# Eight instead of seven head pairs of a linear-attention and mixer kernel in plain float32

## The chip, the cores and the metric

The kernel runs on one core of one Trainium2 chip. The metric is the device time of one execution in microseconds (us). TensorE (PE, with its weight loads as PEld) multiplies matrices, VectorE (DVE), ScalarE (ACT) and GpSimd (POOL) work on elements, and SyncE (SP) issues most of the DMA transfers. Each engine goes through its own instructions in a fixed order; an instruction whose input is not there holds up everything behind it on that engine.

## The reference, cut to what matters

Eight batch entries of 576 tokens, eight heads of 64 channels each. First a linear attention:

```python
def phi(x):                                   # x: q or k, 64 channels per head
    proj = x @ w_phi                          # 64 -> 128 features
    proj = proj - max(abs(proj), axis=-1)     # per token
    return concat([exp(proj), exp(-proj)])    # 256 features
q_p, k_p = phi(q), phi(k)
kv, z = k_p.T @ v, sum(k_p, axis=tokens)
x = (q_p @ kv) / (q_p @ z + 1e-6)             # per head; heads side by side: 512 channels
```

Then a mixer over the result, one batch entry at a time: `u = x + (relu(x.T @ w_tok1) @ w_tok2).T` over the tokens (576 to 256 and back), and `u + relu(u @ w_ch1) @ w_ch2` over the channels (512 to 1536 and back).

## The kernel before

Heads are treated in pairs, two on the 128 partitions, so each batch entry has four pairs and there are 32 in all (0 to 31). Pairs 0 to 3 make up the first batch entry, pairs 4 to 7 the second one.

**Two precisions.** A pair with a number under `PLAIN` (L26) is made in plain float32, where each matmul of the program stands as two MATMUL instructions in the trace. The others are made from float32r parts: a value is written as a rounded high part and a low part (what is left), and a product is the sum of three float32r matmuls (`mm3`, L619 ff.). For such a pair the raw keys and queries are loaded as `raw` and stacked, high part on one half of the partitions, low part on the other (`stack`: ACT copies, POOL subtracts; tiles stk and stq). A projection of 128 tokens is then one matmul of 256 columns, whose halves ACT and DVE add up (tile part). A plain pair is loaded by two transfers of 256 and 320 KB into `pair` tiles (`load_plain`, L665), and a projection is one float32 matmul of 128 columns straight from them. Even pairs use the buffers k0 and k1, odd ones q0 and q1; there is one buffer of each, and stk and stq use the same four. So a plain pair's transfer waits until the pair two before it has been projected.

**Tiles of the attention.** ppk, ppq and ppt are the projections of keys, queries and the last 64 query tokens; mx their largest size, pm the difference, kp and qf the exponentials (qh, ql the parts of the latter). pkv is keys times values. The plain way (`add_kv`, L764) is eighteen matmuls of 104 or 130 columns that leave features on the partitions; the split way (`turn_kv`, L731) is twelve matmuls of 256 columns, a copy kf and four transposes pkt. pt are the transposed query features and pn the numerators and denominators: two matmuls per piece where plain, six where split. A piece is 320 or 256 tokens of one head; the name pn_01 says tokens of the first segment (0), second head (1). Then u is copied out; the denominators go through four small DMAs (few, inv, and u twice) with a reciprocal between them, and POOL multiplies u by u into xt, the input of the mixer.

**The mixer.** `token_mix` (L893) transposes xt (px), splits it (xh, xl), multiplies by w_tok1 (pa, then ah, al) and w_tok2 (ph), and adds to xt, in two halves h of 256 channels, two pairs each; pa_1 and ph_1 are those of the second half. `channel_stream` (L1009) works on blocks of 256 tokens: six rounds of 24 matmuls into h (L961) and 24 into acc (L976) each, 288 matmuls per block and 18 blocks. Blocks 0 and 1 lie inside the first batch entry; block 2 crosses into the second one and starts when that one's token mix is done.

**What sets the order.** Every operation is recorded first, then `arrange` (L275) places them on the engines with a table of costs: keys, queries and token mixing have urgency on TensorE, the channel stream is taken where nothing else is ready. So h and acc matmuls fill whatever the rest leaves.

**PSUM banks of the projections** (`less_max`, L631 ff.): from pair 4 on, keys of either kind use the bank keys. Queries that are split use three buffers with the tag rest; plain ones from the 19th tile on (`BORROWED = 18`) use the one bank h, which the channel stream's h uses too:

```python
elif base == 0 and (nplain["q"] % 2 == 0 or nplain["q"] >= BORROWED):
    ps = ps_h.tile([P, 2, 2, F], F32, tag="h", name=f"pp{name}")
elif kind == "k" or base == 0:
    ps = ps_w.tile([P, 2, 2, F], F32, tag="keys", name=f"pp{name}", bufs=1)
else:
    ps = ps_w.tile([P, 2, 2, F], F32, name=f"pp{name}", **REST)
```

All operations are recorded by one helper, so the profile gives nearly every instruction the line L174; tiles tell them apart.

Of the kernel before, what the change touches and what calls it, by code (L numbers as in the profile page):

```python
# [22 lines left out]
T = 256  # L23
E = 1536
NC_, NE, NT = C // P, E // P, T // P
PLAIN = 7  # L26
OPEN = 4
WIDE = 104
BORROWED = 18
# [449 lines left out]
def mixer_kernel(ctx, tc, qk, qkp, vals, w_phi, w1, w1t, w2, wc1, wc2d, out):  # L479
# [125 lines left out]
    def stack(raw, base, name):  # L605

        out = []
        lo = D - base
        for k, (c, n) in enumerate(((0, 512), (512, 640))):
            t = wk.tile([P, n], F32R, tag=f"{name[0]}{k}", name=f"st{name}{k}", bufs=1)  # L610
            src = raw[base:base + D, c:c + n]
            nc.scalar.copy(t[base:base + D], src)
            nc.gpsimd.tensor_tensor(t[lo:lo + D], src, t[base:base + D].bitcast(F32), op=ALU.subtract)
            out.append(t)
        return out
# [42 lines left out]
    def load(i):  # L658

        raw = wk.tile([P, 2 * S], F32, tag="raw", name=f"raw{i}", bufs=1)  # L660
        lo, hi = (D if i <= PLAIN else 0), (D if i == B * NP else P)
        nc.sync.dma_start(raw[lo:hi], qk[i, lo:hi])
        raws[i] = raw

    def load_plain(i):  # L665

        out = []
        for k, (c, n) in enumerate(((0, 512), (512, 640))):
            t = wk.tile([P, n], F32, tag=f"{'kq'[i % 2]}{k}", name=f"pair{i}{k}", bufs=1)
            nc.sync.dma_start(t, qkp[i, :, c:c + n])  # L670
            out.append(t)
        pairs[i] = out

    def keys():
# [3 lines left out]
        for i in range(B * NP):  # L678
            yield from until(lambda: i < 2 or i - 2 in asked)
            if i < PLAIN:  # L680
                load_plain(i)
# [3 lines left out]
            (nc.sync if i else nc.scalar).dma_start(v_sb.rearrange("p u j d -> p (u j d)"), vals[i])  # L685
            plain = D if i < PLAIN else None
            ts = pairs[i] if i < PLAIN else stack(raws[i], D, f"k{i}")
            for g, us in enumerate(groups if i < PLAIN else blocks):
                pm = less_max(ts, us, f"k{i}_{g}", plain)
# [98 lines left out]
    def sides(i):  # L788
        return (0, 1) if i < 2 * NP else (1, 0)

    def queries():
# [3 lines left out]
        for piece in pieces:  # L795
# [9 lines left out]
            if piece:  # L805
                i, k, j = piece
                if (k, j) == (sides(i)[0], 0):
                    plain = 0 if i < PLAIN else None
                    if i < PLAIN:
# [73 lines left out]
    def until(cond):  # L883
        while not cond():
            yield None
# [236 lines left out]
```

## Time and profile before

| what | value |
|---|---|
| median of three runs | 1110.08 us (1109.37 to 1110.85) |
| the profiled execution's own time | 1109.82 us |
| its span, first to last instruction | 1107.9 us |
| mean granted TensorE clock, share of full speed | 0.998 |
| busy share of the span: PE, PEld | 97%, 92% |
| busy share: DVE, ACT, POOL | 61%, 54%, 49% |
| MATMUL instructions | 8862 |
| last 150 us, from about 950 us on | h and acc alone, PE busy without a break |

A busy TensorE in the profile is not one at its peak: the end of a matmul is modelled and reaches into the next, so that a short break does not show as idle time. How many matmuls start in a stretch, and how far apart, tells more. In the trace float32 matmuls count twice.

### The profile page before, as it was taken

To read this page: it belongs to the slowest core of one execution; us is meant where nothing else is said; L and a number is where in the kernel's file an instruction comes from. 1 tells how busy PE (TensorE), PEld (TensorE's weight loads), DVE (VectorE), ACT (ScalarE), POOL (GpSimd) and SP (SyncE) were. 2 spreads that over 40 slices of the span, in tenths; PEclk is the share of its full clock that TensorE was granted. 3 is DMA by queue.
4 is the path that set the end of the run, shared out by engine and by line. 5 is a ranking of instruction groups with operands and counts; after the bars stand their busy time and mean duration, and the time that the engine had idled before them with its cause. 6 is when DMAs were issued, how large, how long until landed. Compare 5 with 4: busy or idle time off the path is not lost.

```text
span 1107.9 us, 23729 instructions
## 1 busy us (share of the span) xinstructions
PE 1078.4 (97%) x8862; PEld 1020.2 (92%) x8862; DVE 675.4 (61%) x1455; ACT 593.1 (54%) x1632; POOL 542.1 (49%) x678
## 2 busy tenths in 40 slices
PE   7999999989999999999999999999999999999998
PEld 7888988979999999999999999899999899999998
DVE  6898966776766765766767677676766552211111
ACT  5776546656666665666565666666665543111110
POOL 1244556756656655666665666576565633001110
PEclk9999999999999999999999999999999999999999
DMA  6564512121121211202122112122221101000000
GB/s 185 160 198 143 166 37 80 41 63 45 46 60 46 59 30 48 62 28 65 46 64 45 62 46 63 25 45 65 46 64 28 43 18 29 3 20 20 20 20 20
DMA packets 60947, 65.25 MB, mean 59 GB/s; under 512 B 28256, under 2 KB 47840, under 8 KB 60832
## 3 DMA queue, kind: packets, MB, share of 16 engines
q1 hardware_dynamic: 60528, 63.33, 20.8%
q8 instruction: 70, 1.15, 0.4%
q10 hardware_dynamic: 304, 0.40, 0.1%
q14 instruction: 45, 0.37, 0.1%
HBM read 53.97 MB, written 9.58 MB: 57 GB/s over the span
## 4 chain that ended last, share of the span: by engine, by line
PE 81%; DMA 8%; DVE 6%; issue 2%; POOL 2%; ACT 1%; SPq 0%; DVEq 0%; ACTq 0%; POOLq 0%
PE acc L174 24%; PE h L174 23%; PE pn L174 8%; PE pkv L174 7%; PE ph L174 4%; PE pa L174 4%; DMA u<-inv 3%; PE ppk L174 3%; PE ppq L174 3%; PE pt L174 3%; DMA inv<-few 2%; DMA few<-u 2%; PE px L174 1%; DVE bitsc L174 1%; DVE ks L174 1%
## 5 line engine op out<-in xcount | busy, mean ns | idle before, releaser
L174 PE MATMUL acc<-gh,wc 128*128 128x256 f32 x1728 | 331.5, 280 | 1.0 <-ACT gh L174 1.0
L174 PEld LDWEIGHTS acc<-gh,wc 128*128 128x128 f32 x1728 | 273.5, 188 | 2.6 <-ACT gh L174 1.4
L174 PE MATMUL h<-uh,wc_h 128*128 128x256 f32 x864 | 242.3, 280 | 1.0 <-DVE gl L174 1.0
L174 PE MATMUL h<-uh,wc_l 128*128 128x256 f32 x864 | 242.8, 281 | 0.0
L174 PE MATMUL h<-ul,wc_h 128*128 128x256 f32 x864 | 241.2, 279 | 0.3 <-POOL ul L174 0.3
L174 PE MATMUL acc<-gl,wc 128*128 128x256 f32 x864 | 241.4, 280 | 0.0
L174 DVE SCALAR_TENSOR_TENSOR gl<-h,gh 128x512 fp32r<-128x512 f32 x108 | 74.3, 688 | 157.5 <-ACT gh L174 156.7
L174 PEld LDWEIGHTS h<-uh,wc_h 128*128 128x128 f32 x864 | 162.6, 188 | 3.4 <-DVE gl L174 1.6
L174 PEld LDWEIGHTS h<-uh,wc_l 128*128 128x128 f32 x864 | 162.6, 188 | 1.6 <-issue 1.5
L174 PEld LDWEIGHTS h<-ul,wc_h 128*128 128x128 f32 x864 | 162.7, 188 | 1.3 <-issue 0.8
L174 PEld LDWEIGHTS acc<-gl,wc 128*128 128x128 f32 x864 | 162.8, 188 | 0.4 <-issue 0.4
L174 ACT ACTIVATE gh<-h 128x512 fp32r<-128x512 f32 x108 | 64.6, 598 | 152.7 <-PE h L174 151.7
L174 ACT ACTIVATE qf<-pt 128x256 f32<-128x256 f32 (+1 forms) x256 | 103.8, 415 | 53.2 <-PE pt L174 51.6
L174 ACT ACTIVATE kp<-pmk 128x256 f32<-128x256 f32 (+1 forms) x320 | 110.5, 395 | 39.9 <-POOL pmk L174 18.2
L174 POOL TENSOR_TENSOR ul<-xt,uh 128x64 fp32r<-128x64 f32 (+3 forms) x120 | 61.2, 544 | 129.3 <-ACT uh L174 128.5
L174 POOL TENSOR_TENSOR ql<-qf,qh 128x320 fp32r<-128x320 f32 (+1 forms) x100 | 85.1, 851 | 69.3 <-ACT qh L174 62.9
L174 POOL TENSOR_TENSOR pmk<-partk,mxk 128x256 f32<-128x256 f32 (+1 forms) x125 | 82.7, 668 | 53.8 <-DVE mxk L174 39.7
L174 POOL TENSOR_TENSOR xt<-u,u 128x256 f32<-128x256 f32 (+1 forms) x64 | 54.7, 855 | 91.4 <-DMA u<-inv 87.8
L174 PE MATMUL pn<-qh,kv 128*128 128x320 f32 (+1 forms) x400 | 98.1, 299 | 0.2 <-DVE partt L174 0.2
L174 POOL TENSOR_TENSOR stk<-raw,stk 64x512 fp32r<-64x512 f32 (+1 forms) x50 | 71.6, 1447 | 50.5 <-ACT stk L174 48.3
L174 DVE TENSOR_TENSOR ql<-qf,qh 128x320 fp32r<-128x320 f32 (+1 forms) x100 | 66.1, 661 | 39.8 <-ACT qh L174 39.6
L174 DVE TENSOR_TENSOR ks<-ks,kp 128x512 f32<-128x512 f32 (+1 forms) x100 | 80.1, 801 | 9.8 <-ACT kp L174 8.2
(111 smaller groups left out, 2354.1 us busy)
## 6 DMA issues: line engine op xcount, KB each, us to landing
raw<-in_qk SPq DMA_DIRECT2D x24, 576.0 KB, 3.7
rawc<-in_wc SPq DMA_DIRECT2D x24, 512.0 KB, 4.4
v<-in_vals SPq DMA_DIRECT2D x31, 325.0 KB, 4.1
u<-inv SPq DMA_DIRECT2D x64, 80.0 KB, 3.2
u<-inv SPq DMA_DIRECT2D x64, 64.0 KB, 2.8
out_x<-xt SPq DMA_DIRECT2D x16, 192.0 KB, 2.1
out_x<-xt SPq DMA_DIRECT2D x11, 256.0 KB, 2.2
out_x<-xt SPq DMA_DIRECT2D x18, 128.0 KB, 1.9
```

What stands on the lines that cost most here:

```text
L174: return getattr(getattr(nc, self.unit), self.name)(*[real(a) for a in self.args], **{k: real(v) for k, v in self.kw.items()})
```

## The change

One number: `PLAIN` goes from 7 to 8. Pair 7, the last one of the second batch entry, is made in plain float32 as pairs 0 to 6 are.

```diff
@@ -23,7 +23,7 @@
 T = 256
 E = 1536
 NC_, NE, NT = C // P, E // P, T // P
-PLAIN = 7
+PLAIN = 8
 OPEN = 4
 WIDE = 104
 BORROWED = 18
```

It is read in `load` (which half of the first raw tile is fetched: now that of pair 8), in `keys` and `queries` (which way a pair goes), in `turn` and `numerators`, and in the size of the input `qkp`. The raw tile of pair 7 falls away. The planner then places all that follows anew. Rows of the planned order have a tile's name with a running number behind it, which is another one in each of the two kernels.

On TensorE, the place where the second half of the second batch entry is token-mixed (ph_1), before:

```order
L174 MATMUL pn_11_3403<-qh_111_3355,kv_8_3212 128x256
L174 MATMUL pt_00_3414<-ident,pmq_00_3368 128x128 x2
L174 MATMUL pt_00_3414<-ident,pmt_3357 128x128
L174 MATMUL ph_1_0_0_3421<-w_h,ah_1_3405 128x320
L174 MATMUL ph_1_0_0_3421<-w_l,ah_1_3405 128x320
L174 MATMUL ph_1_0_0_3421<-w_h,al_1_3410 128x320
L174 MATMUL ph_1_0_0_3421<-w_h,ah_1_3405 128x320
L174 MATMUL ph_1_0_0_3421<-w_l,ah_1_3405 128x320
L174 MATMUL ph_1_0_0_3421<-w_h,al_1_3410 128x320
L174 MATMUL ph_1_1_0_3436<-w_h,ah_1_3405 128x320
```

and the same place now:

```order
L174 MATMUL ph_1_0_0_3173<-w_h,ah_1_3136 128x320
L174 MATMUL ph_1_0_0_3173<-w_l,ah_1_3136 128x320
L174 MATMUL ph_1_0_0_3173<-w_h,al_1_3153 128x320
L174 MATMUL h_5_3157<-uh_3_2334,wc_h 128x256
L174 MATMUL h_5_3157<-ul_3_2345,wc_h 128x256
L174 MATMUL h_5_3157<-uh_3_2334,wc_l 128x256
L174 MATMUL h_5_3157<-uh_0_2300,wc_h 128x256
L174 MATMUL h_5_3157<-ul_0_2306,wc_h 128x256
L174 MATMUL ph_1_1_0_3201<-w_h,ah_1_3136 128x320
```

Channel matmuls (h, acc) stand among the token mix now. Before, none stands between one acc matmul behind the second pair of transposes (px_1_2) and the last ph_1 matmul. At that last ph_1 matmul the order before has issued 582 channel matmuls, the order now 524. The first transposes of this half (px_1_0) stood 122 TensorE instructions behind the numerators pn_01 of pair 7, now 58; the last ones (px_1_3) stood 62 behind pn_11, now 85.

On TensorE, some fifty rows behind the second projection of pair 5's queries (ppq_10), in the token mix of the second batch entry's first half (px_0, pa_0), before:

```order
L174 MATMUL px_0_2_1838<-ident,xt_1_1417 64x128 x2
L174 MATMUL h_2_1775<-uh_3_1569,wc_l 128x256
L174 MATMUL acc_1_1660<-gh_1_1707,wc_3_1346 128x256
L174 MATMUL acc_1_1660<-gl_1_1723,wc_3_1346 128x256
L174 MATMUL acc_1_1660<-gh_1_1707,wc_3_1346 128x256
L174 MATMUL pa_0_1834<-xl_0_0_1836,w_h 128x256
```

and now:

```order
L174 MATMUL px_0_2_1840<-ident,xt_1_1417 64x128 x2
L174 MATMUL h_2_1777<-uh_3_1569,wc_l 128x256
L174 MATMUL acc_1_1660<-gh_1_1707,wc_3_1346 128x256
L174 MATMUL ppk_0_1850<-wp,pair_1744 128x128 x2
L174 MATMUL pa_0_1836<-xl_0_0_1838,w_h 128x256
```

The first key projection of pair 7 stands here now; before it stood some 155 rows further on, inside the third ph_0 group of the second batch entry. Its third projection, from the second of the two tiles (pair_1888), stands 28 TensorE instructions behind pair 5's last query projection (ppq_11), which frees that buffer; the first one stands 60 behind ppq_10.

On SP, the weights' transfers (rawc), the denominators of pair 5 (few) and, now, the transfers of pair 7; before:

```order
L174 DMA rawc_2_1024_1725<-in_wc 128x512
L174 DMA rawc_3_1024_1791<-in_wc 128x512
L174 DMA few_1_1821<-u_5_1_1812 64x1x4
L174 DMA rawc_10_1840<-in_wc 128x512
L174 DMA rawc_8_1928<-in_wc 128x512
```

and now:

```order
L174 DMA rawc_2_1024_1725<-in_wc 128x512
L174 DMA pair_1744<-in_qkp 128x512
L174 DMA rawc_3_1024_1793<-in_wc 128x512
L174 DMA few_1_1823<-u_5_1_1814 64x1x4
L174 DMA rawc_10_1842<-in_wc 128x512
L174 DMA pair_1888<-in_qkp 128x640
```

The two transfers of pair 7 stand between those of the weights; its first raw transfer, which stood at the start of the queue, is now that of pair 8.

## Rows read from the trace of the kernel before

**Rows 1.** Work in stretches of 25 us, columns in the first line.

```profile
core 0: us, PE busy (x) PEld busy (x) DVE busy (x) ACT busy (x) POOL busy (x), PEclk, DMA share, GB/s
...
125.00:150.00 25.00, 22.52 (x173) 20.82 (x172) 21.16 (x35) 14.04 (x31) 10.32 (x8) 1.00 0.32 91
...
200.00:225.00 25.00, 25.00 (x208) 24.27 (x209) 19.36 (x43) 16.24 (x50) 16.82 (x23) 1.00 0.16 45
225.00:250.00 25.00, 21.18 (x138) 17.06 (x136) 17.20 (x40) 14.60 (x42) 15.98 (x20) 0.93 0.25 60
250.00:275.00 25.00, 24.48 (x205) 22.71 (x204) 14.60 (x35) 16.52 (x48) 15.31 (x20) 1.00 0.16 45
```

**Rows 2.** The same view in stretches of 3 us.

```profile
231.00:234.00 3.00, 2.38 (x17) 1.75 (x15) 2.94 (x9) 2.05 (x7) 1.39 (x2) 1.00 0.70 219
234.00:237.00 3.00, 1.74 (x9) 0.93 (x7) 2.85 (x5) 2.93 (x9) 2.92 (x4) 1.00 0.03 7
237.00:240.00 3.00, 2.33 (x14) 2.16 (x14) 1.90 (x5) 0.12 (x2) 2.84 (x4) 0.79 0.15 23
240.00:243.00 3.00, 3.00 (x17) 3.00 (x16) 1.47 (x3) 1.60 (x4) 0.10 (x1) 0.64 0.47 174
```

**Rows 3.** TensorE in order of time, 220 to 252 us; columns in the first line.

```profile
start us, us, engine line op out<-in xcount [idle before <-releaser]
...
229.98 0.28 PE L174 MATMUL acc<-gh,wc 128*128 128x256 f32 x1
...
235.50 0.83 PE L174 MATMUL px<-ident,xt 128*128 128x128 f32 x4 [0.65 <-ACT qh L174]
...
237.84 0.39 PE L174 MATMUL pa<-xl,w_h 128*128 128x256 f32 x1 [0.67 <-DVE xl L174]
...
246.22 0.28 PE L174 MATMUL h<-uh,wc_h 128*128 128x256 f32 x1
```

**Rows 4.** TensorE in order of time, matmuls of plain pairs, 10 to 62 us.

```profile
15.23 1.71 PE L174 MATMUL pkv<-v,kp 128*128 128x104 f32 x14
...
18.84 1.24 PE L174 MATMUL pn<-qf,kv 128*128 128x320 f32 x4
19.92 0.27 PE L174 MATMUL pt<-ident,pmt 128*128 128x128 f32 x1
...
58.02 0.60 PE L174 MATMUL ppk<-wp,pair 128*128 128x128 f32 x4
58.46 1.03 PE L174 MATMUL pn<-qf,kv 128*128 128x256 f32 x4
59.33 0.38 PE L174 MATMUL pt<-ident,pmq 128*128 128x128 f32 x2
```

**Rows 5.** TensorE in order of time, matmuls of split pairs, 220 to 252 us.

```profile
222.96 0.39 PE L174 MATMUL ppk<-wp,stk 128*128 128x256 f32 x2
...
224.44 0.40 PE L174 MATMUL pn<-qh,kv 128*128 128x256 f32 x2
...
226.98 2.38 PE L174 MATMUL pkv<-kp,v 128*64 128x256 f32 x20
229.19 0.60 PE L174 MATMUL pkv<-ks,ones 128*64 128x256 f32 x4
229.72 0.30 PE L174 MATMUL px<-ident,xt 128*64 128x128 f32 x1
...
230.59 0.66 PE L174 MATMUL pkt<-ident,kf 128*128 128x128 f32 x4 [0.33 <-DVE kf L174]
...
249.07 0.46 PE L174 MATMUL pn<-qh,kv 128*128 128x320 f32 x2
249.36 0.31 PE L174 MATMUL pn<-ql,kv 128*128 128x320 f32 x1
```

**Rows 6.** TensorE's waits in the whole span: us in total, times, longest.

```profile
PE ppq L174 <- DVE gl L174: 1.6, 2, 0.8
```

**Rows 7.** DMA issues of the plain pairs: count, KB each, median us to landing.

```profile
pair<-in_qkp SPq DMA_DIRECT2D x7, 320.0 KB, 3.9
```

## The prediction

> **What bounds the kernel now.** I read the page's busy shares first: PE is busy for 97% of the span, no other engine for more than 61%, so TensorE's order of work is where time is made or lost. Next I read the work by stretches of 25 us. The reader is to look at how many matmuls start, not at the busy time, which a short break doesn't lower. The stretches beside the one I mean start 208 and 205; the stretch 225 to 250 us starts 138 [rows 1]. No other stretch between 25 and 950 us is as poor. At (208 + 205)/2 = 206.5 per 25 us one matmul takes 0.121 us, so the 68.5 that are missing are worth 8.3 us. Cut into 3 us, the hole is deepest from 231 to 243 us: 17 + 9 + 14 + 17 = 57 matmuls where 99 would go, 42 x 0.121 = 5.1 us [rows 2].
>
> TensorE in order of time says why. The last channel matmul starts at 229.98 us and the next one at 246.22 us [rows 3]. For 16.2 us only attention and token mixing of the second batch entry are left, and these wait for one another: px for ACT, pa for DVE [rows 3]. Blocks 0 and 1 hold 2 x 288 = 576 channel matmuls, the order has used 582 by then, and block 2 can't go on before the second batch entry is mixed, whose last pair is pair 7. So the kernel has two regimes: for nearly all of its length the channel stream fills TensorE and a matmul more costs its time; in this one place the filler has run out, and what counts is how early pair 7 is done.
>
> The clock belongs to the same place. It was granted at 0.79 and 0.64 of full speed in 237 to 240 and 240 to 243 us [rows 2], that is at 1.2 GHz instead of 2.4 for part of the time, right behind the emptiest stretches (17 and 9 matmuls). It cost 0.21 x 3 + 0.36 x 3 = 1.7 us, which are part of the 8.3. A hole that is only made shallower gives this part back as a whole or not at all.
>
> **The change part by part.**
>
> *TensorE's own work for pair 7.* Plain, counted as the trace counts: 18 + 18 instructions of projections, 36 of pkv, 8 + 8 of pn. A chain of 14 pkv takes 1.71 us and a single matmul 0.27, so (1.71 - 0.27)/13 = 0.11 each; ppk gives (0.60 - 0.27)/3 = 0.11 as well; four pn of 320 columns go from 18.84 to 19.92 us, 0.27 each; four of 256 from 58.46 to 59.33, 0.218 each [rows 4]. Sum: 72 x 0.11 + 8 x 0.27 + 8 x 0.218 = 7.9 + 2.2 + 1.7 = 11.8 us. Split: 18 projections at 0.39 - 0.28 = 0.11; pkv with its ones from 226.98 to 229.72, 2.74 us; four pkt at (0.66 - 0.27)/3 = 0.13; twelve pn of 320 columns at 0.46 - 0.31 = 0.15 and twelve of 256 at 0.40 - 0.28 = 0.12 [rows 3, 5]. Sum: 2.0 + 2.7 + 0.5 + 1.8 + 1.4 = 8.5 us (with the unrounded parts 8.5). The plain pair costs 3.3 us more on the engine that bounds. From below: of that, up to all may fall into breaks that TensorE has anyway; in 125 to 150 us only 173 matmuls start [rows 1], 33 fewer than in a full stretch, 4 us; so 0 to 3.3. I take 3.3, since the planner puts channel matmuls into most of such breaks, and a plain matmul only pushes them back.
>
> The Trainium skill states in "FP8 and Floating Point Precision", section "TensorE Precision Notes", that true float32 takes four passes through the array. For 104 columns at 2.4 GHz that would be an estimate of 4 x 104/2.4 = 173 ns; the trace has two instructions of 110 ns, 220 ns, as long as the 128 columns of ppk. By the rule pkv would take about 0.8 us less and the extra work would be 2.5 us; the measurement decides, and the sum keeps 3.3.
>
> *The other engines.* DVE loses the additions of the parts, ks, kf and half of ql, POOL stk, stq, pm and half of ql, ACT the part copies and half of the exponentials. None of this bounds (61, 49 and 54% busy) and I price it at nothing in itself. What hides it is the channel stream. DVE is the one to watch: it is busy 21.16 of 25 us at 125 to 150 us [rows 1], where pair 7's reductions and subtractions now come in, and has 3.8 us left there. If that cover is gone, the wait shows on TensorE's ppk and ppq.
>
> *The hole.* Pair 7's first projection moves ahead by 155 rows, and it needs no stack, no sum of parts and no pm on POOL behind it. The order now has h and acc matmuls among ph_1, and 524 used at the end of ph_1 instead of 582, so 52 of blocks 0 and 1 are still there: the filler doesn't run out. If TensorE is as full there as beside it, the 8.3 us come back. From below: nothing, if it stands still all the same (rival B); 5.1 us, if only the deepest part goes. I take 8.3. What is late next is the chain pn, u, few, inv, u, xt, px of pair 7, below.
>
> *Query projections in bank h.* Five more tiles (ppt, four ppq) stand in the bank that the channel stream's h uses. In the whole span ppq waited for DVE's gl, the reader of h, 1.6 us in two waits, 0.8 the longest [rows 6], and until now seven tiles stood there beside running channel work (two of pair 5, five of pair 6). That is 1.6/7 = 0.23 per tile, 5 x 0.23 = 1.1 us. Bounds: 0 to 5 x 0.8 = 4 us. I take 1.1.
>
> *Loads.* The two pair transfers wait for pair 5's last projections to free q0 and q1, and SP waits with them: behind the first stand weights (rawc_3) and the denominators of pair 5 (few), behind the second more of these. A 320 KB one takes 3.9 us to land [rows 7]. Between ppq_10 and the first ppk of pair 7 stand 60 matmuls, 7.3 us: hidden. Between ppq_11 and the third ppk stand 28, 3.4 us, against 0.3 (the end of ppq_11) + 3.9 = 4.2: 0.8 us late, and TensorE waits for it in its order. Bounds: 0, and 0.8 + 3.9 = 4.7 if it stands behind one more transfer of its size. I take 0.8. The raw transfer that goes was of keys alone and landed long ago: nothing.
>
> *Sum.* Against the profiled execution's own 1109.8 us (0.3 under the median, span 1107.9): 1109.8 + 3.3 + 1.1 + 0.8 - 8.3 = 1106.7 us. The largest gain that these bounds allow, extra work and waits at nothing, is 1101.5. The stretches of steady work behind 250 us are planned anew as well; I see no term of either sign there.
>
> **Rivals.**
>
> *B, the hole stays and is only moved.* px_1_0 now stands 58 matmuls behind pn_01, 7.0 us, where it stood 122 behind. In the hole, from pn_11 of pair 7 (224.44) to its px (235.50), this chain took 11.1 us [rows 3, 5]. If it is as long with the engines busy, TensorE waits some 4 us there in its order, filler or not, and may lose its clock again. Against it: the 11.1 were made in a stretch where POOL did stk and stq too, and px_1_3 has 85 matmuls now instead of 62. With nothing recovered the time is 1109.8 + 3.3 + 1.1 + 0.8 = 1115.0 us. It decides the sign from the point where less than 5.2 of the 8.3 come back; where less than 3 do, the kernel is measurably slower. With the 4 us wait alone it is 1110.7.
>
> *C, the gain and the price cancel.* Only the deepest part of the hole goes, 5.1 us: 1109.8 + 5.2 - 5.1 = 1109.9 us. For it: matmuls in the token mix wait for ACT and DVE in every batch entry, and that part doesn't depend on filler. Against it: the neighbouring stretches hold such waits too, and I measured the hole against them.
>
> *D, the extra work is hidden as well.* The plain pair falls into the breaks of 125 to 150 us: 1106.7 - 3.3 = 1103.4 us. For it: 173 matmuls there. Against: DVE is 85% busy there, which is what those breaks wait for.
>
> **How the numbers follow.** A change of 0.2%, 2.2 us, is about what a measurement of this kernel can tell from none. The forecast, hole filled and extra work paid, has 0.42 (own range 1104 to 1108.5); D has 0.13; C, with B's 4 us wait, 0.25; B with little recovered 0.20. Faster by over 0.2% (under 1107.9) takes D and most of the forecast: 0.13 + 0.39 = 0.52. Within 0.2% (to 1112.3) takes C and the rest, and a little of B: 0.27. Slower is the rest of B, 0.21 with what a new plan may cost behind 250 us. Predicted is 1106.7; the range is 1102 to 1114: below it only what exceeds D, above it a B with nothing recovered at all.
>
> **What would show it.** The hole: between the last pn of pair 7 and the end of ph_1 there should be h and acc matmuls, over 195 matmuls in each 25 us (float32 ones counted twice), and the clock at 1.00 in every stretch from 225 to 250 us. B would show as idle time of px behind POOL xt of over 3 us, and a clock below 1.00. The extra work: 36 more instructions of float32 projections, and a pkv of the pair of about 4 us. The bank: ppq's waits for DVE gl at about 2.7 us instead of 1.6. The load: one wait of ppk for the pair's DMA under 1 us. I am wrong if the hole is gone and the time isn't lower by over 2 us: then something given back after 250 us is larger than what I counted.

## The result: 13.3 us faster, four times the gain forecast

Four executions of the changed kernel took 1095.66 to 1098.67 us, median 1097.14; those of the kernel before, run beside them, 1109.37 to 1111.56 us, median 1110.46. The ratio is 0.988, with a 95% interval from 0.9863 to 0.9897. The forecast was 1106.7 us with a range from 1102 to 1114: the direction was right, and the time lies 4.9 us under the low end. The profiled execution took 1095.66 us; its span is 1093.8 us, against 1107.9 us.

The stretches of the changed kernel, to be laid beside [rows 1]; columns as there:

```profile
core 0: us, PE busy (x) PEld busy (x) DVE busy (x) ACT busy (x) POOL busy (x), PEclk, DMA share, GB/s
...
125.00:150.00 25.00, 25.00 (x204) 24.08 (x204) 22.82 (x44) 17.21 (x41) 10.35 (x8) 1.00 0.38 112
...
175.00:200.00 25.00, 24.09 (x172) 20.03 (x171) 13.44 (x31) 12.72 (x34) 9.06 (x11) 1.00 0.12 37
200.00:225.00 25.00, 25.00 (x211) 23.55 (x210) 16.46 (x39) 16.24 (x47) 13.96 (x19) 1.00 0.15 44
225.00:250.00 25.00, 24.77 (x210) 23.33 (x209) 15.84 (x37) 14.56 (x44) 17.22 (x24) 1.00 0.29 71
250.00:275.00 25.00, 25.00 (x214) 23.59 (x213) 16.37 (x38) 16.02 (x45) 14.90 (x18) 1.00 0.17 33
...
231.00:234.00 3.00, 3.00 (x28) 3.00 (x27) 0.95 (x4) 1.78 (x4) 2.92 (x4) 1.00 0.03 1
234.00:237.00 3.00, 3.00 (x27) 2.99 (x26) 0.55 (x1) 1.95 (x6) 2.68 (x4) 1.00 0.17 50
```

The hole is gone: 210 matmuls start from 225 to 250 us where 138 did, 28 and 27 in 3 us where 17 and 9 did [rows 2], and the clock is granted in full. The stretch 125 to 150 us has changed too: 204 matmuls instead of 173. Not all is full: from 175 to 200 us only 172 start (174 before).

TensorE in order of time in the changed kernel, to be laid beside [rows 3 to 5]:

```profile
start us, us, engine line op out<-in xcount [idle before <-releaser]
...
139.80 0.72 PE L174 MATMUL pkv<-v,kp 128*128 128x104 f32 x5
...
142.19 1.28 PE L174 MATMUL pkv<-v,kp 128*128 128x104 f32 x10
...
189.35 0.50 PE L174 MATMUL acc<-gh,wc 128*128 128x256 f32 x2 [0.69 <-ACT gh L174]
190.07 0.71 PE L174 MATMUL ppq<-wp,pair 128*128 128x128 f32 x4 [0.22 <-DVE gl L174]
...
194.64 0.70 PE L174 MATMUL px<-ident,xt 128*128 128x128 f32 x4
...
222.79 0.31 PE L174 MATMUL ph<-w_h,ah 128*128 128x320 f32 x1
...
223.67 0.28 PE L174 MATMUL h<-uh,wc_h 128*128 128x256 f32 x1
...
228.91 0.28 PE L174 MATMUL ph<-w_h,al 128*128 128x256 f32 x1
229.03 0.28 PE L174 MATMUL h<-uh,wc_l 128*128 128x256 f32 x1
```

Channel matmuls (h) now stand among the ph_1 matmuls. The last ph_1 starts at 228.91 us; before, the channel stream could only go on at 246.22 us [rows 3].

**Where the 14.1 us of the span are.** To count what a break costs, I gave every matmul of the order the time that it takes in an unbroken chain (0.1135 us for float32r with 256 columns, 0.1465 with 320, 0.222 for a float32 projection or pkv of two instructions), and laid the orders along the traces. What the clock shows beyond this work is standing. "Work done" is the sum of such times up to a point, which makes the same place comparable in both kernels; the times are those of before.

| work done, us (time before) | standing before | after | difference |
|---|---|---|---|
| 0 to 110 (to 130 us) | 20.1 | 18.8 | -1.3 |
| 110 to 130 (to 155 us) | 4.9 | 0.5 | -4.4 |
| 130 to 160 (to 188 us) | 3.0 | 1.1 | -1.9 |
| 160 to 190 (to 221 us) | 2.6 | 4.4 | +1.8 |
| 190 to 220 (to 262 us): the hole | 11.6 | 1.0 | -10.6 |
| the rest | 56.4 | 55.0 | -1.4 |
| work in all | 1009.3 | 1013.0 | +3.7 |
| span | 1107.9 | 1093.8 | -14.1 |

All values are estimates that rest on these prices; where the edges of a stretch are laid moves one by up to 1 us. So there were two gaps, not one. The first, in the kernel before, columns as above:

```profile
143.00:146.00 3.00, 2.59 (x17) 2.03 (x16) 2.69 (x7) 2.62 (x7) 0.76 (x1) 1.00 0.05 6
146.00:149.00 3.00, 2.29 (x15) 1.65 (x13) 2.96 (x4) 1.61 (x4) 1.32 (x2) 1.00 0.24 44
149.00:152.00 3.00, 2.40 (x19) 2.30 (x20) 1.14 (x4) 1.69 (x5) 1.12 (x2) 1.00 0.01 0
152.00:155.00 3.00, 2.17 (x19) 1.98 (x18) 3.00 (x5) 1.50 (x4) 2.40 (x2) 1.00 0.03 2
```

Here 15 to 19 matmuls start in 3 us, over 12 us on end (eight of them are pn matmuls of 0.27 us, so that not all that is missing is standing). It is the token mix of the second batch entry's first half. The changed kernel has pair 7's keys there, from 127 us on.

### The profile page after: what moved, and what is told of

It reads as the page before. It is cut to its first block, busy times and chain, and to the rows that moved or that the text cites. A ratio compares the mean times of both kernels' runs of the same rounds, so it can differ in the third digit from the quotient of the medians.

```text
span 1093.8 us, 23687 instructions
## 1 busy us (share of the span) xinstructions
PE 1073.7 (98%) x8880; PEld 1023.7 (94%) x8880; DVE 651.7 (60%) x1442; ACT 584.9 (53%) x1613; POOL 526.1 (48%) x660
## 4 chain that ended last, share of the span: by engine, by line
PE 90%; DMA 4%; DVE 2%; POOL 1%; issue 1%; ACT 1%; SPq 0%; ACTq 0%; DVEq 0%; POOLq 0%
PE acc L174 25%; PE h L174 25%; PE pn L174 9%; PE pkv L174 8%; PE ph L174 5%; PE pa L174 5%; PE ppk L174 4%; PE ppq L174 3%; PE pt L174 3%; DMA u<-inv 2%; PE px L174 2%; DMA inv<-few 1%; PE pkt L174 1%; DMA few<-u 1%; POOL ql L174 0%
## 5 line engine op out<-in xcount | busy, mean ns | idle before, releaser
L174 POOL TENSOR_TENSOR ql<-qf,qh 128x256 fp32r<-128x256 f32 (+1 forms) x96 | 81.2, 846 | 73.5 <-ACT qh L174 60.8
L174 POOL TENSOR_TENSOR pmk<-partk,mxk 128x256 f32<-128x256 f32 (+1 forms) x120 | 80.5, 673 | 58.9 <-DVE mxk L174 42.1
L174 PE MATMUL pn<-qh,kv 128*128 128x256 f32 (+1 forms) x384 | 95.0, 298 | 0.5 <-DVE xt L174 0.2
L174 POOL TENSOR_TENSOR stq<-raw,stq 64x512 fp32r<-64x512 f32 (+1 forms) x48 | 71.8, 1495 | 36.1 <-ACT stq L174 26.2
L174 DVE TENSOR_TENSOR ql<-qf,qh 128x256 fp32r<-128x256 f32 (+1 forms) x96 | 61.4, 639 | 41.5 <-ACT qh L174 41.3
L174 POOL TENSOR_TENSOR stk<-raw,stk 64x512 fp32r<-64x512 f32 (+1 forms) x48 | 68.4, 1441 | 32.3 <-ACT stk L174 27.1
```

The source lines that it names most:

```text
L174: return getattr(getattr(nc, self.unit), self.name)(*[real(a) for a in self.args], **{k: real(v) for k, v in self.kw.items()})
```

## The experiments

Each kernel ran beside the kernel before, whose median was 1111.55 us in the first group, 1110.64 in the second and 1111.27 in the third. The question was what makes pair 7 early, and how much of 13.3 us is due to it. One theory (number 1 in the expectations) is the buffer: stacked keys lie in k0 and k1. With seven plain pairs, pair 6 holds these until its queries are projected, so pair 7 can't be stacked earlier. As a plain pair, pair 7 lies in q0 and q1, which pair 5 leaves much earlier. The rows of TensorE and ACT in the kernel before, in order of time, fit that:

```profile
131.48 0.71 PE L174 MATMUL ppq<-wp,pair 128*128 128x128 f32 x4 [0.76 <-DVE gl L174]
...
143.82 1.34 PE L174 MATMUL pn<-qf,kv 128*128 128x320 f32 x4 [0.41 <-ACT qf L174]
...
149.59 0.55 PE L174 MATMUL px<-ident,xt 128*128 128x128 f32 x3 [1.31 <-POOL xt L174]
...
153.93 0.71 PE L174 MATMUL ppq<-wp,pair 128*128 128x128 f32 x4 [0.83 <-DVE gl L174]
...
154.67 0.62 ACT L174 CAST stk<-raw 64x512 fp32r<-64x512 f32 x1 [1.17 <-PE ppq L174]
```

The first copy into stk is released by pair 6's ppq. (The four PE rows with a wait are the waits that the trace shows in the first gap, 3.3 us together; the longest is px, 1.31 us behind xt.) The other theory (number 2) is that the plain way counts, with less for the element engines to do.

**Seven plain pairs, with the two kinds of stacked tile exchanged.** Stacked keys go to q0 and q1, queries to k0 and k1.

```diff
-            t = wk.tile([P, n], F32R, tag=f"{name[0]}{k}", ...)
+            t = wk.tile([P, n], F32R, tag=f"{'qk'[name[0] == 'q']}{k}", ...)
```

> Pair 7 is split as in the kernel before; only the buffers are exchanged: stacked keys lie in q0 and q1, stacked queries in k0 and k1, so that pair 7's keys no longer wait for pair 6's queries to be projected. Theory 1 (the gain comes from when pair 7's keys may start, the plain way is only what put them into the free buffers): the hole at 228 to 246 us is gone and the 3.3 us of plain work are saved, 1097.1 - 3.3 = 1094 us (1091 to 1098). Theory 2 (the gain comes from the plain way itself, with its shorter chain and less work on ACT, POOL and DVE): the hole stays, 1108 to 1112 us.

Measured: 1107.19 us, ratio 0.9953 (0.9933 to 0.9974), in neither theory's range. The row of the stacking copies (duration in ns: least, median, most; first and last start; forms):

```profile
L174 ACT CAST stk<-raw x50: 614/668/727, 121.4 to 835.3; 64x512 fp32r<-64x512 f32 x25, 64x640 fp32r<-64x640 f32 x25
```

and the stretches of this kernel:

```profile
125.00:150.00 25.00, 23.44 (x175) 20.32 (x173) 22.37 (x40) 17.09 (x42) 15.12 (x14) 1.00 0.34 109
150.00:175.00 25.00, 23.73 (x179) 21.03 (x177) 16.64 (x34) 13.19 (x35) 14.48 (x17) 1.00 0.15 40
225.00:250.00 25.00, 25.00 (x209) 23.70 (x208) 16.92 (x41) 16.55 (x49) 17.05 (x24) 1.00 0.25 60
```

Pair 7 is stacked 33 us earlier, and the hole is gone without a plain pair 7 (209 matmuls). This shows the buffer as the cause of the hole. But the gap from 125 to 175 us stays (175 and 179 matmuls), and behind the third batch entry this plan stands 50.7 us up to the eighth, where the kernel before stands 42.6. Of the gain that the theory expected, a third at most came in the time. In the second and third batch entries, counted as in the last table below, the standing falls from 31.7 to 21.7 us; most of that is lost again behind, where pair 7 is long done.

**Eight plain pairs, with pair 7 in k0 and k1.** The plain way without its buffer.

```diff
-            t = wk.tile([P, n], F32, tag=f"{'kq'[i % 2]}{k}", ...)
+            t = wk.tile([P, n], F32, tag=f"{'kqk'[i % 2 + (i == 7)]}{k}", ...)
```

> Pair 7 is plain as in the changed kernel, but loaded into k0 and k1, which pair 6 holds until its queries are projected. Theory 1 (start of the keys): the hole is back, with the plain work on top, 1110.5 + 3.3 = 1113.8 us (1109 to 1117). Theory 2 (the plain way): most of the gain stays, 1097 to 1101 us.

Measured: 1111.51 us, ratio 1.001 (0.9992 to 1.0028). The row of the plain key projections in this kernel:

```profile
L174 PE MATMUL ppk<-wp,pair x144: 270/275/553, 3.9 to 176.2; 128*128 128x128 f32 x144
```

and in the changed kernel:

```profile
L174 PE MATMUL ppk<-wp,pair x144: 270/275/552, 3.8 to 140.7; 128*128 128x128 f32 x144
```

The hole's stretch in this kernel:

```profile
225.00:250.00 25.00, 23.62 (x173) 19.34 (x172) 20.64 (x47) 17.43 (x55) 18.91 (x26) 1.00 0.18 45
```

Pair 7's last key projection comes 35 us later, pair 8 waits for k0 and k1 in its turn, the hole is back (173 matmuls) and the whole gain is gone, as theory 1 said. Without the early buffer the plain way brings nothing; without the plain way the early buffer brings about 4 us of time in these plans.

**Six plain pairs** (`PLAIN = 6`), where pair 6 is split and pair 7's buffers are those of split pairs.

> PLAIN = 6: pairs 6 and 7 are split. The first split pair, 6, has its keys in k0 and k1, which pair 4 left long before. Theory 1 (start of the keys): no hole or a small one and two plain pairs' extra work less than in the changed kernel, 1097.1 - 6.6 = 1090.5 us (1089 to 1099). Theory 2 (the plain way): one pair more that is slow to be done, the hole grows, 1112 to 1125 us.

Measured: 1139.41 us, ratio 1.0264 (1.0233 to 1.0294). Theory 1 had 1090.5 us; it is wrong here by 49 us, and theory 2's 1125 is passed as well. The stretches:

```profile
125.00:150.00 25.00, 21.87 (x166) 19.84 (x164) 24.64 (x37) 15.66 (x36) 15.79 (x14) 1.00 0.51 152
150.00:175.00 25.00, 19.85 (x109) 16.28 (x109) 20.14 (x35) 14.58 (x34) 19.62 (x18) 0.80 0.34 98
```

TensorE's waits in this kernel's whole span (us, times, longest):

```profile
PE px L174 <- POOL xt L174: 8.7, 6, 2.5
PE ppk L174 <- DVE partk L174: 4.6, 6, 1.5
```

DVE has no time left from 125 to 150 us (24.64 of 25), ppk waits for its sums of parts, and px for xt. The buffer isn't all: what a split pair asks of the element engines has no room here.

**Six plain pairs with less conversion of weights.** Left out are two of the DVE operations that convert a piece of the mixer's weights (sign and low bits), so that DVE has room.

```diff
-        nc.vector.scalar_tensor_tensor(m, top, 0x80000000, m, ...)
-        nc.vector.scalar_tensor_tensor(m, low, 29, m, ...)
```

> PLAIN = 6, and the conversion of all weights leaves out its two DVE operations that put in the sign and the low bits, so that DVE has some 50 us less to do before 160 us; the weights are other numbers, all else is as with PLAIN = 6. Theory 3 (PLAIN = 6 is slow because DVE is full with the conversion while split pairs 6 and 7 add work to it): the stretches with few matmuls from 100 to 225 us fill up, 1139 - 25 or more, at most 1114 us. Rival (the chain of two split pairs itself is too long, whatever DVE has to do): 1130 us or more, only the start is quicker.

Measured: 1116.14 us, ratio 1.0073 (1.0051 to 1.0094), 23.3 us under six plain pairs with the whole conversion: 2 us over the most that theory 3 allowed, far from the rival's 1130. Two stretches of it:

```profile
50.00:75.00 25.00, 14.12 (x82) 11.79 (x81) 11.91 (x22) 16.63 (x37) 14.34 (x12) 0.73 0.73 227
...
150.00:175.00 25.00, 25.00 (x187) 21.34 (x186) 17.32 (x39) 17.54 (x49) 14.88 (x18) 1.00 0.16 43
```

There 187 matmuls start instead of 109, and in the second batch entry's token mix TensorE stands 10.6 us instead of 41.2. So a loaded DVE is most of what makes a split pair dear in this place. The plan has a new hole at 50 to 75 us, with the clock at 0.73, so the number says nothing finer.

**Nine plain pairs** (`PLAIN = 9`), first as they are, then with the exchange of the first experiment.

> PLAIN = 9: pair 8 is plain too, which lies behind the hole. It prices a plain pair where the channel stream has work: 1097.1 + 3.3 = 1100.4 us by my term (1099 to 1102). Theory 1 (start of the keys) adds that the first split pair, 9, now has its keys in the buffers of pair 8, as pair 7 had before, so a stretch with few matmuls may come back before the third batch entry's token mix: up to 1108. By theory 2 (the plain way shortens the chain and eases the other engines) it costs nothing or gains: 1094 to 1098.

> PLAIN = 9 with the buffers of stacked keys and queries exchanged, so that the first split pair, 9, has its keys in the buffers that pair 7 left and not in those of pair 8. Theory 1 (what counts is that the first split pair's keys don't wait for the queries of the pair before): the waits that PLAIN = 9 had at the second and third batch entry go, one plain pair more than the changed kernel is left, 1097.1 + 3.5 = 1100.6 us (1098 to 1105). Rival (an odd number or another plan is just worse, whatever the buffers): 1110 to 1116 as with PLAIN = 9.

Measured: 1113.64 us, ratio 1.0034 (1.002 to 1.0047), and with the exchange 1101.49 us, ratio 0.9924 (0.9908 to 0.9939). The first is 5.6 us over the most that theory 1 allowed (1108), the second within its range. Where the first split pair is stacked, with nine as they are:

```profile
L174 ACT CAST stk<-raw x46: 616/668/729, 229.1 to 844.5; 64x512 fp32r<-64x512 f32 x23, 64x640 fp32r<-64x640 f32 x23
```

and with the exchange:

```profile
L174 ACT CAST stk<-raw x46: 614/669/726, 192.8 to 831.7; 64x512 fp32r<-64x512 f32 x23, 64x640 fp32r<-64x640 f32 x23
```

As they are, nine pairs stand 6.9 us in the second batch entry's token mix and 19.1 us in the third entry behind it; with the exchange it is 8.4 and 10.7. The shortage had moved to the next entry, and the buffer takes most of it away.

**Eight plain pairs with the exchange.** Now pair 8's keys would have to wait for q0 and q1, which pair 7 holds.

> PLAIN = 8 as in the changed kernel, with the buffers of stacked keys and queries exchanged: the first split pair, 8, has its keys in the buffers of pair 7, which are held until pair 7's queries are projected. Theory 1: stretches with few matmuls come back around the second and third batch entry's token mix, 1097 + 8 to 1097 + 15 = 1105 to 1112 us. Rival (the plain way of pair 7 makes the gain, buffers don't matter): 1095 to 1099 us.

Measured: 1108.51 us, ratio 0.9991 (0.9969 to 1.0013). The stacking copies in the changed kernel, in this one, and one stretch of this one:

```profile
L174 ACT CAST stk<-raw x48: 616/668/725, 155.0 to 827.8; 64x512 fp32r<-64x512 f32 x24, 64x640 fp32r<-64x640 f32 x24
```

```profile
L174 ACT CAST stk<-raw x48: 614/668/729, 185.0 to 826.7; 64x512 fp32r<-64x512 f32 x24, 64x640 fp32r<-64x640 f32 x24
```

```profile
225.00:250.00 25.00, 23.65 (x174) 20.54 (x175) 20.71 (x46) 16.55 (x49) 18.85 (x22) 1.00 0.24 64
```

The hole is back in part (174 matmuls), with pair 8 stacked 30 us later: the next pair's attention seems to be filler for this place too. For seven, eight and nine pairs together:

| plain pairs | as they are: first stk, median | exchanged: first stk, median |
|---|---|---|
| 7 | 154.7 us, 1111 | 121.4 us, 1107.2 |
| 8 | 155.0 us, 1097.1 | 185.0 us, 1108.5 |
| 9 | 229.1 us, 1113.6 | 192.8 us, 1101.5 |

In each row the kernel whose first split pair is stacked earlier is faster, by 4, 11 and 12 us, whichever way the exchange goes. The 4 us alone would be within what another plan can move (below).

**Pair 7's query projections not in bank h.** The changed kernel, whose last five plain query tiles take the rest buffers.

```diff
-        elif base == 0 and (nplain["q"] % 2 == 0 or nplain["q"] >= BORROWED):
+        elif base == 0 and nplain["q"] < 35 and (nplain["q"] % 2 == 0 or nplain["q"] >= BORROWED):
...
-        elif kind == "k" or base == 0:
+        elif kind == "k" or base == 0 and nplain["q"] < 35:
```

> The changed kernel with one thing undone: pair 7's five query projections stand in the three rest buffers as when they were split, not in the bank h of the channel stream. By the term of my prediction this saves 1.1 us (0 to 4): 1096.0 us. Rival (the bank costs nothing, since the trace of the changed kernel has 0.2 us of ppq waiting for DVE gl): 1097.1 us, up to what another plan brings, 1094 to 1100.

Measured: 1099.47 us, ratio 0.9902 (0.9886 to 0.9919), not the 1096.0 of the prediction's term but within the rival's range. The bank costs nothing that its undoing gives back.

**Two numbers of the planner, with seven and eight pairs.** Each new order is a new plan for the whole kernel, so one time may be a lucky or an unlucky plan. `RATE` (210 to 212) and `FILL` (165 to 168) are numbers in the planner that have nothing to do with pair 7.

```diff
-LANDING, RATE, BEGIN = (1000.0, 1400.0), 210.0, 750.0
+LANDING, RATE, BEGIN = (1000.0, 1400.0), 212.0, 750.0
```

```diff
-FILL = 165.0
+FILL = 168.0
```

> The kernel before with one number of the planner's table changed (the DMA rate it reckons with, 210 to 212), which changes nothing that is computed, only the order. It measures what another plan alone is worth with PLAIN = 7. Theory 1 (buffers): the hole before the second batch entry's token mix stays, 1107 to 1114 us. Rival (the 13 us are mostly luck of the plan): it may come out as low as 1098 us.

> The changed kernel with the same change to the planner's DMA rate, 210 to 212. Theory 1: no hole, 1094 to 1102 us, 8 to 16 us under its partner with PLAIN = 7. Rival (luck of the plan): anywhere from 1097 to 1110 us.

> The kernel before with another number of the planner's table changed (the latency it reckons with behind a matmul, 165 to 168). Theory 1: 1107 to 1114 us with the hole. Rival (luck of the plan): as low as 1098 us.

> The changed kernel with the planner's latency behind a matmul changed from 165 to 168. Theory 1: no hole, 1094 to 1102 us, 8 to 16 us under its partner with PLAIN = 7. Rival (luck of the plan): anywhere from 1097 to 1110 us.

Measured (us), with the standing of each plan, counted as above, in the second batch entry's token mix (from its first px to its last ph) and in the third batch entry behind it:

| plan | 7: median; standing in 2nd, 3rd | 8: median; standing in 2nd, 3rd | 8 less 7 |
|---|---|---|---|
| as it is | 1110.5; 22.5, 9.2 | 1097.1; 9.5, 6.4 | -13.3 |
| RATE 212 | 1106.7; 18.0, 10.3 | 1105.3; 11.4, 7.4 | -1.3 |
| FILL 168 | 1105.3; 19.8, 10.8 | 1102.3; 11.4, 7.3 | -3.0 |

The hole's stretch in the four, in the order of their texts:

```profile
225.00:250.00 25.00, 22.42 (x175) 19.79 (x173) 17.55 (x44) 15.74 (x45) 14.87 (x20) 1.00 0.29 65
```

```profile
100.00:125.00 25.00, 21.66 (x147) 20.39 (x146) 20.96 (x37) 14.41 (x33) 10.16 (x9) 0.86 0.59 170
...
225.00:250.00 25.00, 24.20 (x201) 23.98 (x202) 16.52 (x39) 16.27 (x50) 18.09 (x26) 1.00 0.14 36
```

```profile
225.00:250.00 25.00, 22.38 (x169) 19.33 (x168) 17.85 (x43) 16.09 (x46) 15.05 (x18) 1.00 0.28 70
```

```profile
225.00:250.00 25.00, 24.77 (x206) 23.32 (x205) 17.71 (x41) 16.73 (x53) 17.95 (x26) 1.00 0.18 52
```

In every plan seven pairs have a hole there (138, 175, 169 matmuls) and eight have none (210, 201, 206). In the two places together the standing falls by (31.7 + 28.3 + 30.6)/3 - (15.9 + 18.8 + 18.7)/3 = 30.2 - 17.8 = 12.4 us, against 3.7 us more work: 8.7 us are gained in this part of the kernel. The medians fall by 5.9 us on average, between 1.3 and 13.3. The 8 to 16 us between partners that theory 1 expected came with neither number: 1.3 us can't be told from nothing with executions that spread over 5 us, and for the size of the gain the rival, luck of the plan, holds. All four times lie outside theory 1's ranges, by 0.3 to 3.3 us. The rest of the plan decides the difference: with `RATE` at 212 the eight pairs lose 7.7 us more standing than the changed kernel before 134 us already, where the clock falls to 0.86.

In the two places themselves the buffer counts for more than the plan. Their standing together goes by the exchange from 31.7 to 21.7 us with seven pairs, from 15.9 to 23.2 with eight and from 26.0 to 19.1 with nine, and eight pairs in k0 and k1 stand 30.0; plans of the same kernel differ by 3.4 at most.

The second entry's token mix can be parted once more. In its first half (first px to last ph of that half), where the first gap lies, seven pairs stand 5.9, 5.4 and 5.5 us in the three plans, with the exchange 7.5, and eight pairs in k0 and k1 5.9; eight pairs stand 1.4, 1.2 and 3.3, and with the exchange 1.5. From there to the last ph, where the hole lies, seven pairs stand 16.7, 12.6 and 14.3 us, but with the exchange 7.2, like the 8.1, 10.2 and 8.1 of eight pairs. So the hole asks only that pair 7 be early, whichever way it is made; in these kernels the first gap closes only where pair 7 is early and plain.

## Why the prediction was half right

**The bound and the mechanism: right.** TensorE's order bounds; filler ran out in the second batch entry's mix, and an earlier pair 7 fills it. The prediction's tests came out: h and acc among ph_1, over 195 matmuls and a clock of 1.00 from 225 to 250 us. What it had not seen is why pair 7 was late. It read an order in which pair 7 came 155 rows sooner. The cause is a buffer that pair 6 held, as the first two experiments show. One reading was wrong: in the 16.2 us without channel matmuls there was not only the second batch entry's work. The pkv chain at 226.98 us is pair 8's [rows 5], as is the numerator with kv_8 in the order, so the next pair was filler already; it did not suffice.

**"The 8.3 us come back": mis-sized.** It was 10.6 us. I had measured the hole over 25 us against neighbours, and these held standing too; the stretch from 221 to 262 us stood 11.6 us and stands 1.0 now. The part that the clock had cost, 1.7 us in the prediction, came back whole. The shallower holes of the other kernels (169 to 175 matmuls) keep the clock at 1.00 too; no run shows the "not at all".

**The first gap: the step that failed.** The prediction read 173 matmuls at 125 to 150 us as 4 us missing, and allowed them only as cover for the extra work ("so 0 to 3.3"). It was a second hole: 4.9 us of standing before and 0.5 after, 4.4 us gained and another 1.9 just behind. The bound was drawn at the price of the work that falls into it. But a gap that opens because TensorE waits in its order can close nearly wholly when other instructions are put ahead of the wait. Rival D saw the place and put 3.3 us on it. The argument against it, that those breaks wait for a busy DVE, is true of half of them: of the four waits shown above, two are ppq behind gl, which DVE writes (1.6 us), one is px behind xt of POOL, one pn behind qf of ACT. None is a wait for a step of pair 7. In the changed kernel the trace shows no wait of TensorE between 125 and 175 us. For a plain pair the argument did not hold: DVE is as busy from 125 to 150 us with the split pair 7 of the exchange (22.37 us) as with the plain one (22.82), but TensorE starts 175 matmuls there with the one and 204 with the other (standing: 4.7 us and 1.1), and POOL is busy 15.12 us against 10.35. With the exchange, too, the longest wait in that stretch is a ppq of an earlier pair:

```profile
132.72 0.71 PE L174 MATMUL ppq<-wp,pair 128*128 128x128 f32 x4 [0.88 <-DVE gl L174]
```

So the split pair 7 does not hold TensorE up there by a step of its own that the trace shows; why its instructions do not cover these waits and the plain ones do was not taken apart.

**The extra work of 3.3 us: right.** It is 3.7 us in the orders laid along the trace. The pkv chains above confirm its step of 0.11 us: (1.28 - 0.72)/5 = 0.112. The Trainium skill's four passes for true float32 ("FP8 and Floating Point Precision", section "TensorE Precision Notes") would make it an estimated 2.5 us by the prediction's working; the 3.7 us of the trace do not agree.

**The waits of 1.1 and 0.8 us: wrong, they didn't come.** TensorE's waits in the whole span of the changed kernel:

```profile
PE px L174 <- POOL xt L174: 3.1, 3, 1.5
PE ppq L174 <- DVE gl L174: 0.2, 1, 0.2
```

ppq waits 0.2 us for bank h where the forecast had 2.7, and 1.6 stood before [rows 6]; the experiment with the bank agrees. Both of those waits lie in the first gap, at 131.48 and 153.93 us. The prediction took them for a price of every tile in that bank; they went when the gap closed. No ppk waits for a pair's transfer. SyncE issued the two in time:

```profile
120.09 0.33 SPq L174 DMA_DIRECT2D pair<-in_qkp  x1
130.33 0.33 SPq L174 DMA_DIRECT2D pair<-in_qkp  x1
```

Pair 7's first ppk starts at 127.54 us, 7.4 us behind the first issue, and its third, which needs the second tile, at 134.29, 4.0 us behind the second; the median to landing is 3.6 us here. The prediction had 3.4 us between ppq_11 and this ppk, from 28 instructions at full pace; it was 4.6.

**Rivals B and C: out.** B asked for a wait of px behind xt of over 3 us and a clock below 1.00. The three that there are, 3.1 us together, all lie behind 690 us, the longest is 1.5, and the clock stayed. C had only 5.1 us of the hole go; it was 10.6. A smaller gap did appear, at 183 to 192 us (+1.8 us in the table, with the stretch around it); the longest wait in it is acc's for gh, 0.69 us.

**"No term of either sign there": this is what the range lacked.** For the stretches behind 262 us it is -1.4 us in this pair of plans, so the sum of the chosen plan hardly suffers. But the medians of the third table move by 4 to 8 us from one plan to the next, and only 1 to 3.4 us of standing of that lie in the two places counted there. A range for one plan has to hold that. Put together, against the span's own -14.1 us: the forecast was +3.3 + 1.1 + 0.8 - 8.3 = -3.1. Work is 0.4 more, the waits 1.9 less, the hole 2.3 more, and the rest is what the sum didn't have: the first gap and what lies behind it (-4.4 - 1.9), the new gap (+1.8) and the plan elsewhere (-1.3 - 1.4). In all: -3.1 + 0.4 - 1.9 - 2.3 - 4.4 - 1.9 + 1.8 - 2.7 = -14.1.

**What stays open.** How much eight pairs are worth without the luck of the plan: 8.7 us by the standing in the place itself, 5.9 by the mean of the three medians, whose scatter allows either. The kernel before is the slowest of its three plans and the changed one the fastest of its three, so the rest of the 13.3 us, some 5 to 7, is luck of these two plans. What in the planner's choices makes a later stretch stand more wasn't traced. No kernel that I tried beats the changed one.

## What to carry to other kernels

Where one engine works in order and a stream of filler covers the rest, count the filler and find each place where the starts get thinner; each is a hole with its own price, and what fills it can give back more than the work it costs. Then ask what holds the thing that ends the shortage: here one buffer, shared by two kinds of tile, decided 7 to 10 us of standing. When a planner redoes the whole order, try the change under two or three neighbouring numbers of the planner before believing one time.

## What the runs showed that I had not expected

A planner's number that has nothing to do with the change moves the time by 5 to 8 us: 1111.27 to 1106.66 and 1105.33 us with seven pairs, 1097.14 to 1105.34 and 1102.33 with eight. 25 executions of the kernel before, in the first group, spread from 1106.72 to 1115.66 us, while four executions of the changed one lie within 3 us. And a hole in one stretch can be exchanged for another: with six plain pairs and a lighter DVE the gap at 150 us went and one at 50 to 75 us came, with 82 matmuls and a clock of 0.73.
